# Reading a block's shifted values from memory instead of copying them on chip, and moving one rounding step

## The chip, the cores and the metric

The kernel runs on one core of a Trainium2 chip. Its engines are TensorE (PE; the loads of its weights are listed apart as PEld), VectorE (DVE), ScalarE (ACT), GpSimd (POOL) and SyncE (SP), which only issues requests; sixteen DMA engines move data between HBM and the core's SBUF. The metric is the device time of one execution in microseconds, median of several runs. Before the change it is 612.67 us (three runs, 612.29 to 614.36).

## The reference

The inputs q, k and v have shape 8 x 8 x 576 x 64 (batch, heads, positions, width). The first half is attention in a sliding window: a position sees itself and the 63 before it.

```python
mask = (rel >= 0) & (rel < 64)
scores = np.where(mask, q @ k.T / 8, -1e9)
attn = exp(scores - max) ; attn /= sum + 1e-9
x = (attn @ v)  ->  4608 rows of 512
```

The second half is a mixture of experts on these 4608 rows: a gate (logits from x and a bias by the row's modality) picks one of eight experts for each row, the row goes through that expert's two matrices (512 x 1024, relu, 1024 x 512), and the result is weighted with the gate's probability.

## The kernel before, in words

**Blocks and pairs.** The positions are cut into 72 blocks of 64; a step s of the main loop handles a pair of blocks, 2s and 2s + 1, for all eight heads (36 pairs, and a few steps behind them for what trails). A block's queries see their own block and the block before it. The work of one pair is spread over several steps, and the order on each engine is written out by hand: the loop's calls fix it.

In step s, in this order on the engines:

- TensorE multiplies probabilities with values for pair s - 2 (`values`, L709), VectorE divides by the sums into xa (`values_out`, L717 and L720), and the gate's logits follow for pair s - 3 (L738, VectorE adds the bias into lg at L743).
- TensorE makes the scores of pair s (`scores`, L653). VectorE adds the mask and finds the extreme of each head (`minima`, L667, tiles ss and mn).
- TensorE turns the exponentials of pair s - 1 (`probs_t`, L483), ScalarE copies the turned tile to pT (L688). GpSimd adds a tiny number to the sums (`sums`, L694).
- ScalarE takes the exponentials of pair s (`exps`, L679), two, three and three heads at a time; between them come its copy of the turned xa (xaT, L730), copies of turned keys (L618), and one rounding of an expert's weights (Whi, L114), whose rest VectorE takes (Wlo, L119).

**The values.** `load_v(s)` (L542, or L546 in two halves where a pair crosses two batches) requests the values of pair s into the tile vo, 128 positions x 8 heads x 64. The lower and the upper 64 partitions of vo belong to blocks 2s and 2s + 1. Block 2s + 1 is multiplied with vo as it lies: its own block in the upper half, its predecessor in the lower. Block 2s takes a second tile, ve, whose lower half holds its own block 2s and whose upper half holds its predecessor 2s - 1. `swap_upper(s - 1)` has VectorE copy the upper half of the former pair's vo into it (L556), `swap_v(s - 1)` has GpSimd copy the lower half (L550). Both happen in step s for pair s - 1; `values` reads the result in step s + 1. Two ve tiles take turns, three vo tiles.

**Experts.** From step 5 (`WEIGHTS`) on, the matrices of the two experts that get most rows are fetched in pieces of 256 KB (L103, L107, tile y) and split into a rounded part and a rest. From step 12 (`FIRST`) on, the expert matmuls of finished rows ("slots", L321 and L343) are interleaved with the attention. A generator `it` yields slot work, and `gap(it, True)` lets it advance by one piece; what the piece leaves for other engines is put on a list and issued at the next `run_later()`. For the first slot the rows xt are gathered in step 11 (`load_slot`, L217, five requests, after SyncE has fetched the row number at L204). In step 12 VectorE turns them (`x_turn`, L283). The first piece of the slot leaves `split` on the list: ScalarE rounds to xh (L195), VectorE takes the rest xl (L196).

**Queues.** SyncE issues the requests for v, q, k, weight pieces and gathered rows in program order. Each waits for its buffer. GpSimd issues the scatters of finished rows (L822). The earliest keys and queries land in the tile Whi, which is named so because the rounded weights use it later. The loop is in one large function; these are its lines on the values:

```python
        if 1 <= s < FIRST:
            swap_upper(s - 1)
        if 2 <= s < NPR + 2:
            values(s - 2)
```

Of the kernel before, what the change touches and what calls it, by code (L numbers as in the profile page):

```python
# [8 lines left out]
F32 = mybir.dt.float32  # L9
# [10 lines left out]
P = 128  # L20
W64 = 64
# [5 lines left out]
def tile_window_attn_moe(  # L27
# [12 lines left out]
    nc = tc.nc  # L40
    B, H, S, D = q.shape
# [8 lines left out]
    BPB = S // W64  # L50
# [15 lines left out]
    WEIGHTS = 5  # L66
    FIRST = 12
# [407 lines left out]
    def gap(it, wait=False):  # L475

        if next(it, "end") != "end" and not wait:
            run_later()
            tick()
# [13 lines left out]
    work = actx.enter_context(tc.tile_pool(name="work", bufs=1))  # L493
# [19 lines left out]
    v_v = v.rearrange("b h s d -> b s h d")  # L513
    vo = {}
    ve = {}
# [12 lines left out]
    def turn_bank(s):  # L528

        i = n_tp[0]  # L530
        n_tp[0] += 1
        if s < FIRST and i % 5 > 1:
            return ps_m.tile([P, 512], F32, name=("em", "y0", "y1")[i % 5 - 2])
        return tp_bank()
# [12 lines left out]

    def swap_v(p):

        nc.gpsimd.tensor_copy(out=ve[p][0:W64], in_=vo[p][0:W64])  # L550

    def swap_upper(p):
        if p not in ve:
            ve[p] = work.tile([P, H, D], F32, name="ve", bufs=2)
        if p > 0:
            nc.vector.tensor_copy(out=ve[p][W64:P], in_=vo[p - 1][W64:P])  # L556
# [126 lines left out]
    def probs_t(p, a, pp):  # L683
        ss = st[p, "s"][0][a]
        for hp in range(HP):
            turn(pp[:, hp * P:(hp + 1) * P], ss[:, hp, :])
        pT = work.tile([P, HP * P], F32, name="pT", bufs=2)
        nc.scalar.copy(out=pT, in_=pp)  # L688
        st[p, "p", a] = pT

    def sums(p):
        sm = st[p, "s"][2]
        rs = st[p, "rs"] = small.tile([P, H], F32, name="rs")
        nc.gpsimd.tensor_scalar(out=rs, in0=sm, scalar1=1e-9, scalar2=None, op0=ALU.add)  # L694
# [19 lines left out]
    def values_out(p):  # L714
        rs = st.pop((p, "rs"))
        rw = small.tile([P, 2, 2, HP], F32, name="rw")
        nc.vector.reciprocal(  # L717
            out=rw, in_=rs.rearrange("p (c g) -> p g c", g=2)[:, :, None, :].broadcast_to([P, 2, 2, HP]))
        xa = st[p, "xa"] = xas[p % XBUF]
        nc.vector.tensor_tensor(  # L720
            out=xa[:, 0:DM].rearrange("p (x d) -> p x d", d=R32),
            in0=st.pop((p, "av")).rearrange("p h d -> p (h d)").rearrange("p (x d) -> p x d", d=R32),
            in1=rw.rearrange("p g a c -> p (g a c)")[:, :, None].broadcast_to([P, 2 * H, R32]), op=ALU.mult)
# [193 lines left out]
    it = counted()  # L917
# [15 lines left out]
    def keep_warm(n):  # L933
# [11 lines left out]
        out=brow, in_=mod_bias.rearrange("(o m) e -> o m e", o=1).broadcast_to([P, 2, E]))  # L945
# [19 lines left out]
    for h in range(2):  # L965
# [3 lines left out]
        for m in range(3):  # L969
            nc.gpsimd.affine_select(  # L970
                out=masks[rows, m, own], in_=masks[rows, m, own],
# [4 lines left out]
            else:  # L976
                nc.gpsimd.affine_select(
                    out=masks[rows, m, before], in_=masks[rows, m, before],
# [5 lines left out]
    for t in xas:  # L984
# [4 lines left out]
        out=tri, in_=tri, compare_op=ALU.is_gt, fill=0.0, base=0,  # L989
# [65 lines left out]
    for c in range(NC1):  # L1055
        nc.scalar.dma_start(
            out=wg[c * R32:(c + 1) * R32],
            in_=w_gate[c * P:(c + 1) * P].rearrange("(r d) e -> d r e", d=R32))
# [14 lines left out]
    for s in range(NPR + 4):  # L1073
        j = s % GB
        if s <= FIRST:
            for f, args in at.pop(s, ()):
                f(*args)
        n_tick = 6 if s < FIRST else 5
        n_gap = 0 if s < FIRST else 4
        G = s // GB + 1  # L1080
        heads = PARTS[j] if G < NG else ()
        R = (s - 5) // GB if s >= 5 and j == 1 else -1

        def part(i):
            if not heads:
                return
            if i == 1 and quartered(G):
                turn_heads(G, *heads[1])
                return
            tp = turn_bank(s)  # L1090
            heads_t(G, *heads[i], tp)
            heads_out(tp, G, *heads[i], nc.scalar.copy if heads[i] == K1 else nc.vector.tensor_copy)

        def ranks():
            if R < 0:
                return None
            tp = turn_bank(s)
            rk = route2(R, tp)
            n = None
            if R == NG - 1 or any(R == T for T, _ in EARLY):  # L1100
                n = counts_out(tab if R == NG - 1 else pl, counts(R, tp))
            route3(R, rk)
            return n
# [4 lines that stand above are left out]
            values(s - 2)  # L1108
            if s <= FIRST:
                values_out(s - 2)  # L1110
        if 3 <= s < NPR + 3:
            logits(s - 3, turn_bank(s) if s != FIRST else ps_m.tile([P, 512], F32, name="y0"))
            if (s - 3) % GB == GB - 1:
                route1((s - 3) // GB)
        if FIRST < s < NPR + 2:
            values_out(s - 2)
        if s < NPR:
            scores(s)
            if s == FIRST:
                x_turn(fetched[0])  # L1120
                gap(it, True)
            minima(s)
            if s == FIRST - 2:
                tick(todo[0][-1] - issued[0], table=True)
        if 1 <= s <= NPR:
            if s == FIRST:
                run_later()
            if s >= FIRST:
                swap_upper(s - 1)
            swap_v(s - 1)  # L1130
            for a in range(2):
                probs_t(s - 1, a, turn_bank(s))
            sums(s - 1)
        if s < NPR:
            exps(s, (0, 1))
        if s == 0:
            first_pair(1, (both[:1], both[1:]))
            cast_bias()
        if s <= FIRST:
            if s >= 2:  # L1140
                x_t(s - 2, turn_bank(s) if s != FIRST else ps_m.tile([P, 512], F32, name="y0"))
            run_later()
            tick(2)
            if s < NPR:
                exps(s, (2, 3, 4))
            part(0)
            if s == FIRST:
                weights(s)
                gap(it, True)
            run_later()  # L1150
            tick(n_tick)
            cnt = ranks()
            exps(s, (5, 6, 7))
        else:
            gap(it, True)
            run_later()
            release()
            tick(2)
            if s < NPR:
                exps(s, (2, 3, 4))  # L1160
            if s < FIRST + 4 or s % 2:
                weights(s)
            for f, args in at.pop(s, ()):
                f(*args)
            gap(it, True)
            cnt = ranks()
            if s < NPR + 2:
                x_t(s - 2, turn_bank(s))
            part(0)
            run_later()  # L1170
            tick(n_tick)
            if s < NPR:
                exps(s, (5, 6, 7))
        if n_gap > 2:
            if FIRST <= s < FIRST + 4:
                weights(s)
            gap(it, True)
        part(1)
        run_later()
        tick(n_tick)  # L1180
        if s == WEIGHTS:
            load_weights()
        if s >= WEIGHTS:
            weights(s)
        if n_gap > 3:
            gap(it, True)
        run_later()
        if s == 1:
            select_bias()
        if s == 4:  # L1190
            nc.sync.dma_start(out=xs_blk[DUMMY:DUMMY + 2].rearrange("b p c -> p b c"), in_=padrow)
        for T, xs_ in EARLY:
            if T == R:
                plan(T, xs_, cnt)
# [24 lines left out]
    def pad_rows(e):  # L1219
# [30 lines left out]
        out=few, in_=quarters, scalar=1, op=ALU.bitwise_and))  # L1250
# [114 lines left out]
    with tc.If(trip > 0):  # L1365
        NS = N // P + E
        with ExitStack() as gctx:
# [4 lines left out]
            for st in (1, 2, 4):  # L1372
# [27 lines left out]
                out=eoff, in0=desc[0:1, 0, :], scalar1=-1.0, scalar2=float(E), op0=ALU.mult, op1=ALU.add)  # L1400
# [3 lines left out]
                out=gtab[:, :, 1], in0=rw, scalar1=float(E - 1), scalar2=None, op0=ALU.min)  # L1404

            with tc.For_i(0, trip, 1) as it:
# [8 lines left out]
                    out=xo.rearrange("p (c r d) -> p r c d", r=NR, d=R32), in_=runs_of(xt))  # L1415
# [5 lines left out]
                for c in range(NC1):  # L1421
                    wt = gen.tile([P, F], F32, name="gw1", bufs=2)
                    nc.sync.dma_start(out=wt, in_=w1_v[bass.ds(ee, 1), :, c, :].rearrange("o p f -> (o p) f"))
                    for n in range(F // 512):
                        nc.tensor.matmul(
                            out=hps[n], lhsT=xT[:, c * P:(c + 1) * P], rhs=wt[:, n * 512:(n + 1) * 512],
# [12 lines left out]
                for c2 in range(NC2 // 2):  # L1439
                    wt = gen.tile([P, 2, DM], F32, name="gw2", bufs=2)  # L1440
                    nc.sync.dma_start(
                        out=wt, in_=w2_v[bass.ds(ee, 1), :, 2 * c2:2 * c2 + 2, :].rearrange("o p c f -> (o p) c f"))
                    for i in range(2):
                        c = 2 * c2 + i
                        nc.tensor.matmul(
                            out=yp, lhsT=hT[:, c * P:(c + 1) * P], rhs=wt[:, i, :],
# [3 lines left out]
                    out=y, in0=yp, scalar1=xt[:, DM:DM + 1], scalar2=None, op0=ALU.mult)  # L1450
# [3 lines left out]
                    out=out, out_offset=bass.IndirectOffsetOnAxis(ap=oi, axis=0),  # L1454
                    in_=y, in_offset=None, bounds_check=N - 1, oob_is_err=False)
# [31 lines left out]
```

## Time and profile before

| | |
|---|---|
| median of 3 runs | 612.67 us (612.29 to 614.36) |
| profiled execution | 612.32 us, its span 610.5 us |
| busy: TensorE | 593.4 us, 97% of the span |
| busy: VectorE | 377.3 us, 62% |
| busy: ScalarE | 282.8 us, 46% |
| busy: GpSimd | 138.1 us, 23% |
| read from and written to HBM | 67.36 MB and 23.78 MB |
| steps 5 to 12, by VectorE's rows | about 35 to 84 us |

A step's start can be found in VectorE's rows by its copy into ve (L556): 34.98, 40.21, 45.10, 51.49, 57.20, 63.02 and 70.13 us are steps 5 to 11. In a row of a timeline the numbers are the start and the length in us, then engine, line, operation and tiles (out<-in); a bracket at the end tells how long the engine stood idle before and what released it. In a row of waits the numbers are us in total, times, and the longest. In a row of stretches stand the stretch, its length, and the busy time of PE, PEld, DVE, ACT and POOL with the count of instructions, then the granted clock of TensorE, the busy share of the DMA engines and GB/s.

### The profile page before, as it was taken

Reading aid. Unit: us, or ns where it says so; the run is one execution under the profiler, and the core shown is the slowest. Engines: PE = TensorE matmul, PEld = TensorE weight load, DVE = VectorE, ACT = ScalarE, POOL = GpSimd, SP = SyncE. Lnnn points to the kernel's source line nnn. Section 1 sums busy time; section 2 is a strip of 40 time slices with the busy share of each in tenths; the row PEclk is TensorE's granted clock in tenths of the full one; section 3 lists DMA queues with packets and bytes.
Section 4 is the critical chain, followed back from the end, with each engine's and each line's share of the span. In section 5 each row is a group of like instructions: output and inputs, shape, how many; then the busy total and the mean of one; then the engine's idle time right before and its main releaser. Section 6 shows DMA issues by size and latency. Waiting matters only on the chain.

```text
span 610.5 us, 17234 instructions
## 1 busy us (share of the span) xinstructions
PE 593.4 (97%) x6281; PEld 527.8 (86%) x6281; DVE 377.3 (62%) x1479; ACT 282.8 (46%) x907; POOL 138.1 (23%) x313
## 2 busy tenths in 40 slices
PE   8999889999999999999999999999999999999996
PEld 5888778889898898989898899899999999999983
DVE  3899988878777877678656465323224634765311
ACT  3899876666656564636462211111113522653110
POOL 6333332142312311321323131011001111102102
PEclk7999999999999999999999999999999999999999
DMA  9999866686776845554513033632152553687301
GB/s 171 214 237 235 209 178 169 154 196 157 192 167 153 210 108 125 145 132 82 137 53 107 36 103 122 180 116 70 34 173 77 166 172 103 202 250 253 117 18 39
DMA packets 175655, 87.95 MB, mean 144 GB/s; under 512 B 139802, under 2 KB 158288, under 8 KB 175440
## 3 DMA queue, kind: packets, MB, share of 16 engines
q1 hardware_dynamic: 166992, 67.33, 45.2%
q0 software_dynamic: 5840, 18.92, 8.4%
q8 instruction: 50, 0.82, 0.6%
q10 hardware_dynamic: 2736, 0.58, 0.5%
q14 instruction: 37, 0.30, 0.2%
HBM read 67.36 MB, written 23.78 MB: 149 GB/s over the span
## 4 chain that ended last, share of the span: by engine, by line
PE 76%; DVE 5%; ACT 2%; issue 1%; SPq 1%; DMA 1%; POOL 0%; POOLq 0%; DVEq 0%; ACTq 0%
PE y L343 29%; PE em L321 21%; PE sp L321 10%; PE tp L483 7%; PE av L709 3%; PE sp L653 3%; PE tp L738 1%; DVE xt L283 1%; ACT ss L679 1%; DVE xl L196 1%; DMA xs_scratch<-xa,idx 1%; SPq L603 1%; PE tp L393 1%; PE em L368 1%; DVE ss L667 0%
## 5 line engine op out<-in xcount | busy, mean ns | idle before, releaser
L343 PE MATMUL y<-Whi,hh 128*128 128x512 f32 x288 | 115.8, 402 | 0.0
L679 ACT ACTIVATE ss<-ss,mn 128x128 f32<-128x128 f32 x288 | 112.3, 398 | 3.5 <-DMA y<-in_moe_modality_id_dram 2.6
L343 PE MATMUL y<-Wlo,hh 128*128 128x512 f32 x288 | 112.7, 391 | 0.0
L343 PE MATMUL y<-Whi,hl 128*128 128x512 f32 x288 | 112.4, 390 | 0.0
L354 POOL DMA_INDIRECT out_dram<-y,id x36 | 38.7, 1076 | 218.3 <-DVE y L351 159.9
L330 DVE SCALAR_TENSOR_TENSOR hl<-em,hh 128x512 fp32r<-128x512 f32 x50 | 34.5, 691 | 83.9 <-ACT hh L329 83.5
L321 PE MATMUL em<-xh,Whi 128*128 128x256 f32 x400 | 81.7, 285 | 0.0
L321 PE MATMUL em<-xl,Whi 128*128 128x256 f32 x400 | 79.2, 279 | 0.0
L321 PE MATMUL em<-xh,Wlo 128*128 128x256 f32 x400 | 79.1, 279 | 0.0
L329 ACT ACTIVATE hh<-em 128x512 fp32r<-128x512 f32 x50 | 30.0, 599 | 105.1 <-PE em L321 100.1
L688 ACT COPY pT<-tp 128x512 f32<-128x512 f32 x57 | 31.2, 590 | 75.8 <-PE tp L483 75.8
L667 DVE CUSTOM_DVE_ANT_0 ss<-sp,masks 128x128 f32<-128x128 f32 x288 | 63.4, 285 | 2.4 <-PE sp L653 2.4
L321 PEld LDWEIGHTS em<-xh,Whi 128*128 128x128 f32 x400 | 62.8, 188 | 2.3
L343 PEld LDWEIGHTS y<-Whi,hl 128*128 128x128 f32 x288 | 54.1, 188 | 12.0
L343 PEld LDWEIGHTS y<-Whi,hh 128*128 128x128 f32 x288 | 54.2, 188 | 9.5 <-issue 0.8
L343 PEld LDWEIGHTS y<-Wlo,hh 128*128 128x128 f32 x288 | 54.3, 188 | 8.4
L321 PEld LDWEIGHTS em<-xh,Wlo 128*128 128x128 f32 x400 | 60.9, 188 | 0.0
L321 PEld LDWEIGHTS em<-xl,Whi 128*128 128x128 f32 x400 | 60.9, 188 | 0.0
L822 POOL DMA_INDIRECT xs_scratch<-xa,idx x36 | 36.4, 1012 | 90.5 <-DVE e_n_p L154 30.8
L679 ACT ACTIVATION_READ_ACCUMULATOR ss<-ss,mn 128x1 f32 x288 | 56.4, 196 | 0.0
L329 ACT ACTIVATE hh<-sp 128x512 fp32r<-128x512 f32 x22 | 13.2, 598 | 80.4 <-PE sp L321 80.4
L709 PEld LDWEIGHTS av<-ve,pT 128*64 128x64 f32 x576 | 36.3, 138 | 13.1 <-issue 7.8
(239 smaller groups left out, 1146.1 us busy)
## 6 DMA issues: line engine op xcount, KB each, us to landing
xt<-xs_scratch SPq DMA_DIRECT2D x72, 128.0 KB
vo<-in_v_dram SPq DMA_DIRECT2D x32, 256.0 KB
y<-in_moe_w_dram SPq DMA_DIRECT2D x32, 256.0 KB
vo<-in_moe_w_dram SPq DMA_DIRECT2D x18, 256.0 KB
ss<-in_moe_w_dram SPq DMA_DIRECT2D x18, 256.0 KB
xs_scratch<-xs_scratch SPq DMA_DIRECT2D x8, 514.0 KB
pT<-in_moe_w_dram SPq DMA_DIRECT2D x12, 256.0 KB
qk<-in_k_dram SPq DMA_DIRECT2D x22, 128.0 KB
```

The lines of the kernel that those rows point to most:

```text
L321: nc.tensor.matmul(out=hb[:, i * TP:(i + 1) * TP], lhsT=w[buf][:, c0:c0 + P], rhs=x[:, c * TP:(c + 1) * TP], start=(n == 0), stop=(n == le ...
L329: nc.scalar.activation(out=hh, in_=hb, func=AF.Relu),
L330: nc.vector.scalar_tensor_tensor(out=hl, in0=hb, scalar=0.0, in1=hh.bitcast(F32), op0=ALU.max, op1=ALU.subtract)))
L343: nc.tensor.matmul(out=sl["y", t], lhsT=h[:, i * TP + t * P:i * TP + (t + 1) * P], rhs=w[buf][:, c0:c0 + DM], start=(k == 0 and n == 0), s ...
L354: ins = nc.gpsimd.indirect_dma_start(out=out, out_offset=bass.IndirectOffsetOnAxis(ap=sl["id"][:, t:t + 1], axis=0), in_=y, in_offset=None ...
L483: nc.tensor.transpose(out=out_, in_=in_, identity=ident[p0:p0 + n, p0:p0 + n])
L653: nc.tensor.matmul(out=sp[a][c * W64:(c + 1) * W64, hp * P:(hp + 1) * P], lhsT=qT[rows, place(g + c, hp), :], rhs=kT[rows, win(c, hp), :], ...
L667: nc.vector.tensor_tensor_reduce(out=ss[a][:, hp, :], in0=sp[a][:, hp * P:(hp + 1) * P], in1=mask, scale=-1.0 / 8.0, scalar=3.0e38, op0=AL ...
L679: nc.scalar.activation(out=ss[a][:, hp, :], in_=ss[a][:, hp, :], func=AF.Exp, bias=mn[:, h:h + 1], scale=-1.0, accum_out=sm[:, h:h + 1])
L688: nc.scalar.copy(out=pT, in_=pp)
L709: nc.tensor.matmul(out=by_block(av)[c * W64:(c + 1) * W64, a, :, hp, :], lhsT=pT[:, i:i + W64], rhs=(vo if c else ve)[p][:, 2 * hp + a, :] ...
L822: ins = nc.gpsimd.indirect_dma_start(out=xs, out_offset=bass.IndirectOffsetOnAxis(ap=idx[:, j:j + 1], axis=0), in_=xg[j], in_offset=None)
```

## The change

In steps 5 to 11 a new function `load_ve(s)` allocates ve of pair s already in step s, right behind `values(s - 2)`, and has SyncE request both halves from HBM: block 2s into the lower 64 partitions, block 2s - 1 into the upper. For these seven pairs `swap_upper` and `swap_v` do nothing. The two tiles ve take turns as before, so the request waits until TensorE has read the former contents, in `values(s - 2)`.

In step 12 the first advance of the slots, `gap(it, True)`, moves from ahead of `minima` to behind `probs_t`. The rounding that it leaves on the list is then issued at a later `run_later()`.

```diff
     def swap_v(p):
 
+        if p in loaded:
+            return
         nc.gpsimd.tensor_copy(out=ve[p][0:W64], in_=vo[p][0:W64])
 
+    loaded = []
+
+    def load_ve(p):
+
+        ve[p] = work.tile([P, H, D], F32, name="ve", bufs=2)
+        for i, g in enumerate((2 * p, 2 * p - 1)):
+            s0 = (g % BPB) * W64
+            nc.sync.dma_start(out=ve[p][i * W64:(i + 1) * W64], in_=v_v[g // BPB, s0:s0 + W64])
+        loaded.append(p)
+
     def swap_upper(p):
+        if p in loaded:
+            return
         if p not in ve:
             ve[p] = work.tile([P, H, D], F32, name="ve", bufs=2)
...
             if s <= FIRST:
                 values_out(s - 2)
+            if WEIGHTS <= s < FIRST:
+                load_ve(s)
...
             if s == FIRST:
                 x_turn(fetched[0])
-                gap(it, True)
             minima(s)
...
             for a in range(2):
                 probs_t(s - 1, a, turn_bank(s))
+            if s == FIRST:
+                gap(it, True)
             sums(s - 1)
```

Two places show how the order of instructions moves. The first is SyncE's queue in steps 10 and 11, up to the first of the five requests for the gathered rows xt. (Rows into Whi are keys, rows into y weight pieces; the changed kernel's lines are 14 to 17 further down.) Before:

```order
L542 DMA vo<-in_v_dram 128x8x64
L597 DMA Whi_64<-in_k_dram 128x8x64 x2
L103 ISA
L103 DMA y<-in_moe_w_dram 128x512
L542 DMA vo<-in_v_dram 128x8x64
L204 TENSOR_LOAD rows_1490
L204 ISA x2
L217 ISA
L217 DMA xt<-xs_scratch 32x8x128
```

Changed:

```order
L542 DMA vo<-in_v_dram 128x8x64
L611 DMA Whi_64<-in_k_dram 128x8x64 x2
L561 DMA ve<-in_v_dram 64x8x64 x2
L103 ISA
L103 DMA y<-in_moe_w_dram 128x512
L542 DMA vo<-in_v_dram 128x8x64
L204 TENSOR_LOAD rows_1493
L204 ISA x2
L217 ISA
L217 DMA xt<-xs_scratch 32x8x128
```

The pair of requests for ve comes in ahead of the weight piece, and with it ahead of everything that follows on this queue: the next vo, the row number and xt. The same happens in each of steps 5 to 11.

The second place is ScalarE at the start of step 12. Before:

```order
L114 CAST Whi_65<-y 128x512
L195 CAST xh<-xt 128x512 x2
L688 COPY pT<-tp_1859 128x512
L688 COPY pT<-tp_1866 128x512
L679 ACTIVATE ss,sm<-ss,mn 128x128 x2
L730 COPY xaT<-y_1877 128x512
L679 ACTIVATE ss,sm<-ss,mn 128x128 x3
```

Changed:

```order
L114 CAST Whi_65<-y 128x512
L702 COPY pT<-tp_1849 128x512
L702 COPY pT<-tp_1856 128x512
L693 ACTIVATE ss,sm<-ss,mn 128x128 x2
L744 COPY xaT<-y_1869 128x512
L195 CAST xh<-xt 128x512 x2
L693 ACTIVATE ss,sm<-ss,mn 128x128 x3
```

The two roundings to xh move behind the two copies of turned probabilities, two exponentials and the copy xaT. On VectorE seven copies into ve are gone (steps 6 to 12), and on GpSimd seven.

## The prediction

> **What bounds the kernel now.** I read the page first, then the busy time by stretches, then the waits of the engines in the stretch that the change edits.
>
> ```profile
> PE 593.4 (97%) x6281; PEld 527.8 (86%) x6281; DVE 377.3 (62%) x1479; ACT 282.8 (46%) x907; POOL 138.1 (23%) x313
> 34.00:63.00 29.00, 27.61 (x588) 24.96 (x584) 27.39 (x153) 28.92 (x118) 8.92 (x18) 1.00 0.98 235
> 63.00:78.00 15.00, 11.99 (x215) 10.36 (x215) 14.30 (x72) 11.56 (x43) 6.63 (x11) 1.00 0.86 213
> 80.00:100.00 20.00, 19.60 (x272) 17.75 (x271) 16.74 (x68) 14.92 (x52) 2.50 (x5) 1.00 0.60 152
> ```
>
> TensorE is busy 593.4 of 610.5 us, and from 80 us on it is nearly full. Over the whole span ScalarE and VectorE look idle; that average misleads. The columns of the stretches are PE, PEld, DVE, ACT, POOL, the granted clock, the DMA share and GB/s. From 34 to 63 us (steps 5 to 9) ScalarE works 28.92 of 29.00 us: it is the bound. From 63 to 78 us (steps 10 to 12) VectorE works 14.30 of 15.00 and ScalarE only 11.56: there VectorE is the bound, and TensorE loses 3 us. Whatever these two stretches gain brings the full part forward, so it should reach the end almost whole; the part after 80 us is only shifted.
>
> The waits of ScalarE from 63 to 79 us say where it stands still, and two timelines show the last place:
>
> ```profile
> ACT xh L195 <- DVE xt L283: 1.9, 1, 1.9
> ACT ss L679 <- DVE mn L667: 0.9, 2, 0.7
> ACT ex L769 <- DVE lg L766: 0.5, 1, 0.5
> 75.56 0.60 ACT L114 CAST Whi<-y 128x512 fp32r<-128x512 f32 x1
> 78.12 1.14 ACT L195 CAST xh<-xt 128x512 fp32r<-128x512 f32 x2 [1.95 <-DVE xt L283]
> 79.16 1.06 ACT L688 COPY pT<-tp 128x512 f32<-128x512 f32 x2
> 80.12 0.41 ACT L679 ACTIVATE ss<-ss,mn 128x128 f32<-128x128 f32 x1
> 80.90 0.57 ACT L730 COPY xaT<-y 128x512 f32<-128x512 f32 x1
> 81.37 0.41 ACT L679 ACTIVATE ss<-ss,mn 128x128 f32<-128x128 f32 x1
> ...
> 70.13 0.42 DVE L556 COPY ve<-vo 64x512 f32<-64x512 f32 x1
> 76.72 0.15 DVE L743 TENSOR_TENSOR lg<-y,bias_sel 128x8 f32<-128x8 f32 x1
> 76.79 1.29 DVE L283 STREAM_TRANSPOSE xt<-xt 128x512 f32<-128x512 f32 x2
> 78.01 0.25 DVE L667 CUSTOM_DVE_ANT_0 ss<-sp,masks 128x128 f32<-128x128 f32 x1
> ```
>
> The three waits make 1.9 + 0.9 + 0.5 = 3.3 us, all for VectorE. This is the most that taking work from VectorE can bring. The gathered rows xt were there in time: VectorE turned them at 76.79 straight behind lg, with no wait.
>
> The third resource is the DMA. The rows are single stretches, and SyncE's requests:
>
> ```profile
> 20.00:34.00 14.00, 13.21 (x246) 11.89 (x248) 12.02 (x66) 12.54 (x51) 6.25 (x12) 1.00 1.01 232
> 37.00:39.00 2.00, 2.00 (x30) 1.82 (x29) 2.00 (x15) 2.00 (x8) 0.27 (x2) 1.00 0.58 103
> 39.00:69.00 30.00, 27.59 (x583) 24.71 (x579) 28.28 (x158) 28.99 (x117) 12.33 (x22) 1.00 1.01 252
> 42.00:46.00 4.00, 3.23 (x67) 2.97 (x69) 3.70 (x23) 4.00 (x17) 2.89 (x6) 1.00 1.11 282
> 69.00:71.00 2.00, 1.15 (x15) 0.85 (x8) 1.78 (x8) 2.00 (x6) 1.13 (x2) 1.00 0.14 30
> 71.00:76.00 5.00, 3.92 (x87) 3.61 (x91) 5.00 (x30) 4.32 (x19) 0.00 (x0) 1.00 0.93 208
> DMA packets 17943, 7.57 MB, mean 252 GB/s; under 512 B 16698, under 2 KB 16698, under 8 KB 17935
> 54.47 5.23 SPq L597 DMA_DIRECT2D Whi<-in_q_dram  x4
> 65.49 0.37 SPq L542 DMA_DIRECT2D vo<-in_v_dram  x1
> 69.74 2.52 SPq L217 DMA_DIRECT2D xt<-xs_scratch  x5
> 86.13 1.31 SPq L546 DMA_DIRECT2D vo<-in_v_dram  x2
> ```
>
> The DMA engines are full from 39 to 69 us: 7.57 MB in 30 us, 252 GB/s (the packet row is of that window). SyncE feels it: four requests of L597 take 5.23 us at 54.47. There are two holes: a share of 0.58 from 37 to 39 us, and 0.14 from 69 to 71, which leaves 2 x 0.86 = 1.7 us of room just ahead of the requests for xt.
>
> **The change part by part.** *Copies.* Seven half-tile copies leave each of two engines:
>
> ```profile
> L550 POOL COPY ve<-vo x36: 604/612/1048, 14.5 to 312.8; 64x512 f32<-64x512 f32 x36
> L556 DVE COPY ve<-vo x35: 424/425/532, 20.1 to 324.6; 64x512 f32<-64x512 f32 x35
> PE av L709 <- POOL ve L550: 2.4, 4, 0.8
> ```
>
> VectorE loses 7 x 0.425 = 3.0 us, GpSimd 7 x 0.612 = 4.3 us. In steps 6 to 9 the VectorE copies buy nothing directly, because ScalarE is full there; they let VectorE run ahead. TensorE's waits for GpSimd's copy (2.4 us from 20 to 80 us) cost nothing for the same reason. Before the turn of xt at 76.79 lie six copies. The three of steps 9 to 11 fall into a stretch where VectorE waits for nothing (1.3 us), the earlier three can at most double that. So VectorE would be ready to turn xt between 76.79 - 2.55 = 74.2 and 76.79 - 1.3 = 75.5, and the waits for mn and lg (1.4 us) go away.
>
> *Probabilities ahead of rounding.* In step 12 ScalarE now copies pT twice, does two exponentials and xaT, and only then rounds xh. The pT copies no longer wait for xt. If xt were turned at the same 76.79, the minima would start at 78.01 as now. An exponential can follow its minimum by 0.38 us, as in step 11:
>
> ```profile
> 71.61 0.28 DVE L667 CUSTOM_DVE_ANT_0 ss<-sp,masks 128x128 f32<-128x128 f32 x1
> 71.99 0.40 ACT L679 ACTIVATE ss<-ss,mn 128x128 f32<-128x128 f32 x1 [0.68 <-DVE mn L667]
> ```
>
> That is 78.39; then two exponentials (80.12 to 80.90, 0.78 us), xaT (0.47) and xh (78.12 to 79.16, 1.04) put the third exponential at 80.68 in place of 81.37: 0.7 us gained. VectorE's rounding of xl moves behind xh, to about 80.2, against 79.67 now; the copy that it no longer makes behind it (0.425) nearly pays for that.
>
> *The new requests.* Each of steps 5 to 11 reads two halves of 128 KB, 262 KB in rows of 256 B. A request of 64 rows costs SyncE 1.31 / 2 = 0.65 us (86.13), against 0.37 for a whole vo: 1.3 us a step, hidden while SyncE only waits for the DMA engines. The pair waits for TensorE's products of step s - 2, which stand early in step s; behind it on SyncE wait a weight piece and the next vo, both of which are used steps later. So the wait itself costs nothing; the bytes do. Six pairs lie ahead of xt. The pair of step 5 meets a hole, left by SyncE's table reads; five pairs, 1.31 MB, fall into the full stretch. Their price has two ends:
> - If the engines held the 282 GB/s of 42 to 46 us throughout, 7.57 + 1.31 = 8.88 MB would take 31.5 us in place of 30. The 1.5 us fit into the 1.7 us of room, and xt is not late.
> - At the 232 GB/s of 20 to 34 us, where nearly all is rows of 256 B, 1.31 MB takes 5.6 us; less 1.7 us of room, xt is 3.9 us late, and 5.6 late if the room is lost because SyncE first fetches the row number and then issues five requests.
>
> I take 3.5 us (1.31 MB at the mean of 252 GB/s is 5.2, less 1.7): the added rows are the short ones, and 282 stands for 4 of 30 us. xt is four requests of 131 KB; the DMA took it up at 71 us, and 0.52 MB at the 208 GB/s of 71 to 76 us takes 2.5 us, so now it lands near 74 (an estimate). 3.5 us later is 77.5, and the turn starts at 77.7 or so, 0.9 us after the present one.
>
> [...]
>
> *Sum.* The turn of xt comes 0.9 us later, the new order gives 0.7 back, and I add 0.2 us for a weight piece or a pair that comes late behind it: +0.4 us. The profiled execution took 612.32 us for its span of 610.5, and lies 0.35 us under the median of 612.67; so 612.7 for it, **613.0 us** as a median. The saving of 2 to 3 us on VectorE is exchanged for a wait for xt.
>
> **The rivals.** *The DMA takes it* (faster). The engines have shown 282 GB/s, scatters and reads overlapping. Then the turn starts between 74.2 and 75.5, 1.3 to 2.6 us early, and with 0.7 from the order the gain is 2.0 to 3.3: 609.4 to 610.7, say 610.0. Against it: the full share over 30 us, and SyncE's stretched requests.
>
> *The pair itself is late at TensorE* (slower). Products of step s need the pair of step s - 2, requested last in its step. In step 10 they run at 60.35, and there is no slack behind them:
>
> ```profile
> 60.35 0.27 PE L709 MATMUL av<-ve,pT 128*64 128x64 f32 x1
> 61.85 1.10 PE L653 MATMUL sp<-kT,qT 64*64 64x128 f32 x32
> 62.88 0.66 PE L483 MATMUL em<-ident_r,ss 128*128 128x128 f32 x4
> 63.58 0.59 ACT L688 COPY pT<-em 128x512 f32<-128x512 f32 x1
> ```
>
> TensorE's queue runs products, scores and turns back to back to 63.5, and ScalarE copies pT at 63.58. Every microsecond that the pair of step 8 lands after 60.35 is one of ScalarE's, the bound there. Its place on SyncE is just ahead of the weight piece of 53.51, and the full queue shows 5.0 us from request to landing:
>
> ```profile
> 53.51 0.37 SPq L107 DMA_DIRECT2D y<-in_moe_w_dram  x1
> xs_scratch<-xa,idx POOLq DMA_INDIRECT x6, 5.0
> ```
>
> The pairs of steps 6 and 7 push it by 2 x 262 KB / 232 = 2.3 us, so it lands near 53.5 + 2.3 + 5.0 = 60.8 (an estimate): about on time, and this case decides if it comes 1 us later still. If steps 10 and 11 lose 1 us each and xt is 4 to 5 us late, the result is near +2.5: 615.2. Against it: it needs the low rate throughout.
>
> *Given back later* (no change). The chain of waits goes at 103.63 through a scatter, whose rows the next gather reads:
>
> ```profile
> 103.63 4.14 DMA xs_scratch<-xa,idx
> ```
>
> If that second gather were held by DMA alone, a gain at step 12 would turn into TensorE idling near 118: within 0.5 us of 612.7. Against it: the scatter itself waits for earlier work that would shift along.
>
> **How the numbers follow.** Chances: my forecast 0.40 (its own range 611.2 to 614.6), the DMA takes it 0.25, the late pair 0.24, given back 0.11. A difference under 0.3% (1.8 us, so from 610.8 to 614.5) can't be told from no change here. The forecast and the fourth case lie almost wholly inside; the second gives faster, the third mostly slower. With the edges: faster 0.26, same 0.50, slower 0.24. The range takes in most of both sides: 610.0 to 615.3.
>
> **What would show it.** Right: VectorE idle before L283 (its new line the same) in step 12, ended by the DMA of xt; no wait of ScalarE for mn and lg in steps 10 and 11, but one for mn in step 12; a DMA share near 1.0 through 69 to 71 us; the exponentials directly behind pT. Wrong, faster: the turn of xt before 75.5 with no wait, and over 270 GB/s from 39 to 70. Wrong, slower: TensorE waiting for the DMA of ve before L709's products in steps 9 to 12, and ScalarE's pT copies waiting for TensorE. A wait later than 100 us that was not there before would speak for the fourth case.

## The result and the profile after

The changed kernel takes 620.21 us (median of four runs, 618.42 to 622.6) against 612.98 before: a ratio of 1.0117, 95% interval 1.007 to 1.0165. It is slower by 7.2 us, outside the predicted range of 610.0 to 615.3. The profiled execution took 618.42 us, its span 616.6.

The page's first part and the same three stretches as before:

```profile
PE 592.3 (96%) x6281; PEld 527.0 (85%) x6281; DVE 373.8 (61%) x1472; ACT 282.8 (46%) x907; POOL 132.6 (22%) x306
34.00:63.00 29.00, 22.67 (x455) 20.71 (x454) 21.27 (x131) 24.15 (x95) 6.24 (x14) 1.00 0.91 218
63.00:78.00 15.00, 10.95 (x201) 9.97 (x199) 10.90 (x67) 10.46 (x42) 2.88 (x6) 0.89 1.03 252
80.00:100.00 20.00, 18.11 (x252) 16.48 (x248) 17.98 (x76) 17.97 (x63) 5.71 (x11) 1.00 0.77 193
```

VectorE lost its 3 us of copies (377.3 to 373.8). But from 34 to 63 us, where ScalarE was full with 28.92 of 29.00 us, it now works only 24.15, and TensorE fell from 27.61 to 22.67: both stand waiting. With more asked of it the DMA moved less, 218 GB/s where before had 235, and its engines were less full, a share of 0.91 in place of 0.98. TensorE's waits from 30 to 125 us, and the three places in its timeline, say for what:

```profile
PE av L723 <- DMA ve<-in_v_dram: 5.9, 2, 4.0
PE av L723 <- ACT ss L693: 3.1, 1, 3.1
...
50.76 0.24 PE L723 MATMUL av<-ve,pT 128*64 128x64 f32 x1 [1.92 <-DMA ve<-in_v_dram]
58.83 0.24 PE L723 MATMUL av<-ve,pT 128*64 128x64 f32 x1 [3.13 <-ACT ss L693]
72.90 0.24 PE L723 MATMUL av<-ve,pT 128*64 128x64 f32 x1 [3.95 <-DMA ve<-in_v_dram]
```

These are the products of steps 8, 9 and 11, which read the pairs requested in steps 6, 7 and 9: 9.0 us of standing still. The second names ScalarE, but ScalarE had finished long before and the pair landed 0.14 us ahead of the products, so it is a DMA too (the case of a wait for several things, put down to the wrong one). ScalarE's waits from 45 to 90 us are the same stalls, passed on:

```profile
ACT pT L702 <- PE y L483: 6.8, 2, 4.5
ACT pT L702 <- PE tp L483: 2.3, 1, 2.3
ACT ss L693 <- DVE mn L681: 0.4, 2, 0.2
```

The old waits for VectorE (3.3 us for xt, mn and lg) have shrunk to 0.4 for mn. SyncE's requests and VectorE's turn of xt show the other side:

```profile
41.01 5.03 SPq L611 DMA_DIRECT2D Whi<-in_k_dram  x2
46.15 1.41 SPq L561 DMA_DIRECT2D ve<-in_v_dram  x2
76.64 3.28 SPq L217 DMA_DIRECT2D xt<-xs_scratch  x5
...
82.42 0.15 DVE L757 TENSOR_TENSOR lg<-y,bias_sel 128x8 f32<-128x8 f32 x1
82.49 1.29 DVE L283 STREAM_TRANSPOSE xt<-xt 128x512 f32<-128x512 f32 x2
```

The rows xt are requested 6.9 us later than before (76.64 against 69.74), but VectorE turns them without a wait, straight behind lg: by then the whole program is late. (The profiles do not start alike: ahead of any edit, step 5 begins 1.24 us earlier in the change than in before's, at 33.74 against 34.98. Positions are compared here without taking that off.) The pair of step 6 stands behind two key requests that SyncE needs 5.03 us to hand over, and is asked for at 46.15, 4.6 us ahead of the products that it holds up.

### The profile page after: what moved, and what is told of

Read it like the earlier page. It is cut to its first block, busy times and chain, and to the rows that moved or that the text cites. A ratio compares the mean times of both kernels' runs of the same rounds, so it can differ in the third digit from the quotient of the medians.

```text
span 616.6 us, 17235 instructions
## 1 busy us (share of the span) xinstructions
PE 592.3 (96%) x6281; PEld 527.0 (85%) x6281; DVE 373.8 (61%) x1472; ACT 282.8 (46%) x907; POOL 132.6 (22%) x306
## 4 chain that ended last, share of the span: by engine, by line
PE 79%; DVE 4%; ACT 1%; issue 1%; DMA 1%; POOL 0%; POOLq 0%; SPq 0%; DVEq 0%; ACTq 0%
PE y L343 30%; PE em L321 22%; PE sp L321 10%; PE tp L483 7%; PE av L723 4%; PE sp L667 3%; PE tp L752 2%; DVE xt L283 1%; DVE xl L196 1%; PE tp L393 1%; PE em L368 1%; ACT ss L693 1%; DMA qk<-in_k_dram 1%; DVE ss L681 1%; ACT xaT L744 0%
## 5 line engine op out<-in xcount | busy, mean ns | idle before, releaser
L723 PE MATMUL av<-ve,pT 128*64 128x64 f32 x576 | 41.1, 225 | 9.9 <-DMA ve<-in_v_dram 5.9
```

The source lines that it names most:

```text
L723: nc.tensor.matmul(out=by_block(av)[c * W64:(c + 1) * W64, a, :, hp, :], lhsT=pT[:, i:i + W64], rhs=(vo if c else ve)[p][:, 2 * hp + a, :] ...
```

## The experiments

Each kernel was compared with the kernel before on the same chip. Unless said otherwise its base is before, or the change's requests alone.

| | median us | ratio to before (95%) |
|---|---|---|
| e1 requests, old order | 622.0 | 1.0137 (1.0116 to 1.0158) |
| e2 new order, copies kept | 615.8 | 1.0031 (1.0019 to 1.0043) |
| e3 no copies, no requests | 691.44 | not comparable with before |
| e5 e3 and unread requests | 700.98 | not comparable with before |
| f1 before and six unread pairs | 624.22 | 1.0162 (1.0135 to 1.0189) |
| f4 requests a step earlier | 621.4 | 1.0122 (1.0094 to 1.015) |
| f5 upper halves only | 617.95 | 1.007 (1.0051 to 1.0088) |
| f6 copies to GpSimd | 618.97 | 1.0081 (1.0067 to 1.0095) |
| g1 the change, TensorE kept busy | 621.91 | 1.0144 (1.0115 to 1.0173) |
| g2 e2, TensorE kept busy | 614.08 | 1.0009 (0.9997 to 1.002) |
| g3 six unread pairs, 2 KB rows | 617.15 | 1.0066 (1.0042 to 1.0089) |
| f3 last two pairs only | 614.03 | 1.0014 (0.9997 to 1.003) |
| h1 f3, TensorE kept busy | 613.08 | 1.0 (0.9986 to 1.0013) |
| h2 before, TensorE kept busy | 613.55 | 1.0005 (0.9991 to 1.0018) |
| h3 upper halves out of SBUF | 620.2 | 1.0113 (1.0094 to 1.0131) |
| h4 before, busier start | 613.87 | 1.0011 (1.0001 to 1.0021) |

**The two halves of the change apart.** e1 takes the change with `gap(it, True)` back ahead of `minima`; e2 is the kernel before with only that line moved:

```diff
             if s == FIRST:
                 x_turn(fetched[0])
-                gap(it, True)
             minima(s)
...
             sums(s - 1)
+            if s == FIRST:
+                gap(it, True)
```

> Only the requests for ve in steps 5 to 11; the first advance of the slots stays ahead of the minima. Late-pair theory (TensorE stands in front of the products until the pair lands; 9.0 us of such waits in the changed profile): within 1 us of the changed kernel, 619 to 621.5. Theory that the moved advance costs: 616 or less.

> Only the moved advance in step 12; all values copied as before. By the prediction's term 0.7 us are gained: 612.0 to 612.6 where before is 612.98, that is, hardly to be told from no change. Theory that the moved advance costs: 616 or more.

The requests alone cost what the whole change costs (the intervals of e1 and of the change overlap). The new order alone loses 1.9 us. The two do not add up to the change's 7.2 us; why the second is not seen on top of the first is not shown.

**The bytes without the reader.** Both have the change's order. In e3 nothing is copied or read for steps 5 to 11, and the even blocks use vo; in e5 the pairs are requested on top, into ve tiles that nobody reads. Both leave out the right values of those blocks, and with other values the gate sends rows to other experts, which makes all that comes later another program: they are compared with each other only.

```diff
     def load_ve(p):
-        ve[p] = work.tile([P, H, D], F32, name="ve", bufs=2)
-        ...
+        ve[p] = vo[p]
         loaded.append(p)
```

> Leaves out part of the computation: in steps 5 to 11 neither copies nor requests; block 2s is multiplied with vo as it lies, so its values come out for the wrong positions. The moved advance is kept. What taking the copies away is worth with no bytes in exchange: by the waits of ScalarE for VectorE (3.3 us before) 609.5 to 610.5. If the copies were never on the path: 612 to 613.

> As the kernel with neither copies nor requests, but the seven pairs are requested at the same place of the queue into the two tiles ve, where nobody reads them; block 2s again takes vo as it lies. Late-pair theory: the bytes alone cost little, no more than 1.5 us over the kernel with neither, 610 to 612. Theory that the bytes delay everything on the queue (keys, weight pieces, gathered rows): 616 or more.

Unread pairs cost 9.5 us, and in e5 VectorE stands 8.6 us for xt. f1 shows the same with all values right: the kernel before, its copies and its order, and beside them the pairs of steps 5 to 10 into the tile xt, which lies idle until step 11.

```diff
+        t = idle_x[0][:, p % 2, 0:H * D].rearrange("p (h d) -> p h d", d=D)
+        for i, g in enumerate((2 * p, 2 * p - 1)):
+            s0 = (g % BPB) * W64
+            nc.sync.dma_start(out=t[i * W64:(i + 1) * W64], in_=v_v[g // BPB, s0:s0 + W64])
```

> The kernel before with its copies, in the old order, plus the pairs of steps 5 to 10 requested as in the change but into memory that nobody reads; all values as in the reference. If the bytes are the price (the DMA engines are full from 39 to 69 us, and whatever is next in need of the queue pays), the rows xt land late and TensorE stands still at steps 11 to 13: 5 to 9 us slower, 619 to 623 us, with no wait at the products. If the price is only that the pair itself comes late for its products, an unread pair costs nothing: 613 to 615 us.

10.3 us, more than the change itself. The first to pay are the readers of vo, which stands on the queue behind the unread pair: GpSimd's copies wait 16.0 us for it, and TensorE 6.6 us for these copies, where before has 1.6 (GpSimd's waits from 30 to 84 us, TensorE's from 30 to 125 us in f1 and then before). Then xt is late; the rows are SyncE's request, VectorE's turn and the DMA's packets from 39 to 78 us:

```profile
POOL ve L550 <- DMA vo<-in_v_dram: 16.0, 5, 6.7
PE av L720 <- POOL ve L550: 6.6, 5, 2.5
PE av L709 <- POOL ve L550: 1.6, 3, 0.8
...
78.86 2.64 SPq L217 DMA_DIRECT2D xt<-xs_scratch  x5
86.20 1.30 DVE L283 STREAM_TRANSPOSE xt<-xt 128x512 f32<-128x512 f32 x2 [7.13 <-DMA xt<-xs_scratch]
DMA packets 23303, 8.90 MB, mean 228 GB/s; under 512 B 22065, under 2 KB 22065, under 8 KB 23294
```

xt is requested 9.1 us later than before and VectorE stands 7.13 us for it. Of the 9.1 us f1 itself adds about 0.9 (an estimate): the unread pairs lie in xt's place, so the request for xt has to wait for them. From handing over vo to the request for xt SyncE stood 1.91 us in f1 and 2.19 in g3 below, where the change stood 1.05; e5, whose pairs lie in the tiles ve, stood 1.46. So the loss does not need anyone to read the pairs: the late pair is the place where the change pays, and without it whatever stands behind the pairs on the queue is late.

The 10.3 us are not all transfer. Behind the wait for xt TensorE's granted clock is 0.50, also where it is full:

```profile
90.00:94.00 4.00, 4.00 (x21) 4.00 (x20) 3.80 (x11) 4.00 (x19) 0.33 (x2) 0.50 0.01 2
```

How much of f1's price, and of e5's, is this clock was not measured.

**Earlier requests.** f4 reads all seven pairs, but asks for those of steps 6 to 9 one step earlier, two of them into xt's halves:

```diff
-            if WEIGHTS <= s < FIRST:
-                load_ve(s)
+            for p in {5: (5, 6), 6: (7,), 7: (8,), 8: (9,), 10: (10,), 11: (11,)}.get(s, ()):
+                load_ve(p)
```

> All seven pairs are read, old order, but those of steps 6 to 9 are requested one step earlier, into two more places (the idle halves of xt for 6 and 7). If lateness of the pair at the products is the price, TensorE's waits for ve (9 us in the changed kernel) fall below 2 us and the time is 611 to 614 us. If the bytes are the price, the waits at the products go, but a wait for xt or for keys comes in their place, and the time stays at 619 to 623 us.

The waits for ve in steps 8 to 11 went (two of 1.8 us in all remained there for vo). One for the pair of step 10, not asked for earlier, and one for xt came instead (TensorE's row, then VectorE's), and the time stayed:

```profile
PE av L730 <- DMA ve<-in_v_dram: 3.4, 1, 3.4
...
DVE xt L283 <- DMA xt<-xs_scratch: 4.0, 1, 4.0
```

**Half the bytes, and long rows.** f5 reads only the upper halves and leaves GpSimd its copies. g3 is f1 with the same bytes in rows of 2 KB:

```diff
-        for i, g in ((0, 2 * p), (1, 2 * p - 1)):
+        for i, g in ((1, 2 * p - 1),):
```

```diff
+            out=t, in_=v[p % 8].rearrange("h s d -> (h s d)")[0:P * H * D].rearrange("(p c) -> p c", p=P))
```

> Only the upper half of each pair of steps 5 to 11 is read (131 KB, one request); GpSimd's copy of the lower half stays; old order. If the price goes with the bytes beyond the room in the queue, it is half or less: 2 to 4 us slower than before, 615 to 617.5 us, with waits for ve of 1 to 4 us. If it goes with the waiting request of a step rather than its size, it is as in the version with the loads alone: 620 to 622 us.

> As the version with six unread pairs and the copies kept (624.2 us), but each pair's 262 KB is read in rows of 2 KB by one request of 128 rows instead of two requests with rows of 256 B. If the number of short rows sets the price, it shrinks to a third or less: 614 to 617 us. If the bytes set it, it stays at 620 to 625 us.

Half the bytes cost 4.0 us. The long rows cost 3.9 where the short ones cost 10.3, so the same number of bytes has no fixed price. What sets it is not told apart: g3 also asks with one request a pair where f1 asks with two, and reads other places of v. Of the pairs of steps 9 and 10, SyncE hands over g3's two requests in 1.31 us in all and f1's four in 3.78, and f5, with six requests of short rows and half the bytes ahead of xt, lost as much as g3 (4.0 against 3.9). The length of the rows and the number of requests both fit. SyncE's request for xt and the packets from 39 to 76 us in g3:

```profile
75.92 2.50 SPq L217 DMA_DIRECT2D xt<-xs_scratch  x5
DMA packets 19598, 9.42 MB, mean 255 GB/s; under 512 B 17548, under 2 KB 17548, under 8 KB 19589
```

With long rows the mean rate holds (255 GB/s, before 252); with short ones it drops to 228. But f1's engines were also less full in that stretch, a share of 0.95 against 0.99 in g3 and 1.01 before.

**Only the last pairs.** f3 requests the pairs of steps 10 and 11 alone (`if FIRST - 2 <= s < FIRST`).

> Only the pairs of steps 10 and 11 are read, old order; the copies of steps 5 to 9 stay. At the price that six unread pairs showed (10.3 us for 1.57 MB, 1.7 us a pair) two pairs cost 3.4 us, less what VectorE's relief brings (1 to 2 us): 614.5 to 617 us. If the prediction's room of 1.7 us from 69 to 71 us takes them up, nothing is lost and VectorE's relief shows: 611 to 613.5 us.

No difference can be told. SyncE's requests:

```profile
64.09 1.87 SPq L561 DMA_DIRECT2D ve<-in_v_dram  x2
66.97 0.18 SPq L542 DMA_DIRECT2D vo<-in_v_dram  x1
71.01 2.52 SPq L217 DMA_DIRECT2D xt<-xs_scratch  x5
74.78 1.51 SPq L561 DMA_DIRECT2D ve<-in_v_dram  x2
```

Only the pair of step 10 stands ahead of xt; that of step 11 comes behind it. xt is requested 1.3 us later than before, but SyncE had handed over all that stands ahead of it by 67.15 us and then stood for 3.86. Before stood 3.88 at the same place, 2.1 of it for VectorE's lg ahead of the row number and 1.1 for a scatter; what f3 stood for is not told apart.

**TensorE's clock.** In the changed kernel the granted clock is 0.57 from 74 to 78 us, behind the 3.95 us stall; in e2 it falls too, to 0.68 from 84 to 88 us, behind a wait of 1.85. (The stretches of the change, then of e2, then of before.)

```profile
70.00:74.00 4.00, 1.10 (x39) 1.14 (x39) 2.04 (x9) 2.97 (x13) 0.42 (x2) 1.00 1.04 253
74.00:78.00 4.00, 4.00 (x59) 3.65 (x55) 2.23 (x15) 0.53 (x1) 0.00 (x0) 0.57 1.05 253
```

```profile
80.00:84.00 4.00, 2.34 (x12) 1.90 (x13) 2.76 (x8) 4.00 (x16) 1.02 (x2) 0.89 0.45 170
84.00:88.00 4.00, 4.00 (x47) 3.87 (x48) 2.81 (x9) 3.22 (x10) 0.28 (x1) 0.68 0.38 105
```

```profile
76.00:80.00 4.00, 2.14 (x34) 1.73 (x25) 3.91 (x22) 2.05 (x5) 3.52 (x8) 1.00 0.97 303
84.00:88.00 4.00, 3.60 (x88) 3.17 (x85) 2.93 (x7) 3.04 (x8) 0.34 (x1) 1.00 0.65 187
```

g1 and g2 fill the stalls with matmuls on constants, whose result is overwritten (in g1 also 4, 8 and 12 ahead of the products of steps 8, 9 and 11):

```diff
             hb = sl["hb"]
+            if k == i == 0 and not warmed:
+                warmed.append(1)
+                for _ in range(8):
+                    nc.tensor.matmul(out=hb, lhsT=ones, rhs=ones[:, None, :].broadcast_to([P, 4, P]), ...)
```

> The version with the new order alone and 8 matmuls on constants in front of the first expert matmuls of step 12, where TensorE waits for xh from 79.8 to 81.7 us and the granted clock then is 0.50 from 83.4 to 86.8 us. If the half clock is what makes the new order 1.9 us slower than before, the time is that of before, 613.5 to 614.5 us. If it is the later xh itself (1.5 us later first matmul), it stays at 615.3 to 616.3 us.

> The changed kernel with matmuls on constants in TensorE's stalls, so that the granted clock does not fall after them: 4, 8 and 12 in front of the products of steps 8, 9 and 11, and 8 in front of the first expert matmuls of step 12. In the changed kernel's trace TensorE stands still for 3.95 us before step 11's products and then runs at a granted clock of 0.50 to 0.67 from 74 to 78 us; the version with the loads alone shows three such stretches of 3.4 us. If that is a part of the loss, these stretches go and the time falls by 1.7 to 4 us, to 616 to 618.5 us. If the clock's fall costs nothing (TensorE is not the bound there), it stays at 619.5 to 622 us.

g2 keeps the full clock and is level with before: by the two ratios the half clock was about 1.3 of the 1.9 us that the new order lost. Its stretch, to be set beside e2's:

```profile
84.00:88.00 4.00, 4.00 (x94) 3.73 (x92) 3.14 (x10) 3.22 (x11) 0.73 (x1) 1.00 0.46 120
```

g1 has the full clock (1.00) from 34 to 100 us as well and is no faster than the change. So the half clock is not what the change lost, unless the constants, which took 7.6 us of TensorE, cost as much as they saved.

The same filling, seven matmuls ahead of `part(0)` in step 12, on f3 (h1) and on before (h2, the control):

> The version that reads only the pairs of steps 10 and 11 (614.0 us, level with before), with 7 matmuls on constants in TensorE's stall of step 12 (77.7 to 79.6 us). Its trace had half the clock from 80.2 to 87.8 us, with TensorE full. If that hides the gain of VectorE's relief, the time falls to 611 to 612.5 us; if the two pairs give no gain in the first place, it stays at 613.5 to 614.5 us.

> The control: the kernel before with the same 7 matmuls on constants. Its trace had the full clock after that stall, so there is nothing to win, and the matmuls fit into the stall: 613 to 614 us, within 0.2% of before.

f3's profile had the clock at 0.57 from 80 to 88 us, h1's has 1.00. h1 is level with before and with its control: what two pairs cost and what VectorE's relief of two copies brings come to nothing together, within 0.14%. A small price and a small gain that cancel would look the same.

**Two other ways to relieve VectorE.** f6 gives the upper copies of blocks 9 to 11 to GpSimd; h3, on h2, gives them to a DMA out of vo in SBUF.

```diff
-            nc.vector.tensor_copy(out=ve[p][W64:P], in_=vo[p - 1][W64:P])
+            copy = nc.gpsimd.tensor_copy if 9 <= p < FIRST else nc.vector.tensor_copy
+            copy(out=ve[p][W64:P], in_=vo[p - 1][W64:P])
```

(h3: `nc.sync.dma_start` in place of `nc.gpsimd.tensor_copy`.)

> No bytes at all: in blocks 9 to 11 the copy of the upper half goes to GpSimd instead of VectorE (0.61 us in place of 0.43), everything else as before. It measures what VectorE's relief alone is worth in steps 10 to 12. By the prediction's first step, VectorE reaches the turn of xt up to 1.3 us earlier: 611.0 to 612.5 us beside 613 before. If GpSimd's second copy is late for the products or VectorE is not the bound there: 613 to 614 us.

> The control, with the upper halves of blocks 9 to 11 copied by a DMA out of vo in SBUF (64 rows of 2 KB, 131 KB a step) instead of by VectorE; GpSimd's copies stay. 0.26 MB before xt at the 255 GB/s of the version with long rows is 1.0 us, within the room of 1.7 us. If VectorE's relief is worth something: 611.5 to 612.8 us; if not, or if the DMA is late for the products: 613.3 to 615 us.

Both are slower, and in both copies come late. In f6 GpSimd's first copy runs 3.49 us behind two scatters that it had issued, by its row released by a scatter's transfer; TensorE stands 5.00 us (its row), and the clock is then at 0.50:

```profile
68.77 0.61 POOL L557 COPY ve<-vo 64x512 f32<-64x512 f32 x1 [3.49 <-DMA xs_scratch<-xa,idx]
...
70.09 0.37 PE L710 MATMUL av<-ve,pT 128*64 128x64 f32 x1 [5.00 <-POOL ve L550]
...
70.00:74.00 4.00, 3.91 (x72) 3.88 (x76) 1.11 (x3) 0.00 (x0) 1.90 (x6) 0.50 0.76 177
```

In h3 it is the DMA, although the bytes are few and xt is requested only 1.2 us later than before (TensorE's waits, two of them, then SyncE's request):

```profile
PE av L710 <- DMA ve<-vo: 6.7, 2, 3.4
...
70.96 2.53 SPq L217 DMA_DIRECT2D xt<-xs_scratch  x5
```

So late operands alone can cost nearly as much as the change lost (ratios of 1.0081 and 1.0113 against 1.0117); h3's request comes one step before its use, the change's two. Neither kernel says what VectorE's relief is worth by itself.

**The start.** h4 gives before 7 in place of 3 matmuls on constants at the start (`WARM = 8, 7`).

> The kernel before with 7 instead of 3 matmuls on constants in the stall at 6.4 us. Its trace had half the clock from 8.8 to 15.5 us. If that stretch is the reason that the changed kernel's profile, with the full clock there, was 1.2 us ahead in step 2, the median falls by 0.5 to 1.2 us, to 612.2 to 613.2 us; if the matmuls are in the way or the clock does not matter there, it stays at 613.5 to 614.5 us.

Not faster. In its profile the low clock moved from 8 to 16 us (before 0.58 and 0.56 in its two halves) to 16 to 20 us (0.58), and another came from 80 to 84 us (0.60, before 1.00); so what the clock at the start is worth stays open.

## Why the prediction was wrong

**The price of the bytes: the step that failed.** I took five pairs at the mean of 252 GB/s, less 1.7 us of room: xt 3.5 us late. Measured, its request came 6.9 us late in the change, and with six unread pairs 9.1 us (f1), with the time 10.3 us longer. Three things were off. The rate: I priced the added bytes alone, but the whole stretch moved more slowly, 230 GB/s in the change by the next row; 7.57 + 1.31 MB at that rate take 38.6 us in place of 30 (an estimate). Part of this is that the mixture with the added rows runs lower: f4's engines were full from 39 to 77 us (a share of 1.00) and moved 233 GB/s. Part is that the engines stood: their share was 0.93 in the change and 0.95 in f1, against 1.01 before. The count: I left out the pair of step 5 for a hole; the rule below fits better with it in, which is argued and not shown. The unit: counted in packets, the stretches agree better than in bytes. Before, 17943 packets took 30 us, 598 a microsecond; f1 598 (23303 in 39), and the change, from 39 to 76 us:

```profile
DMA packets 22398, 8.52 MB, mean 230 GB/s; under 512 B 21236, under 2 KB 21236, under 8 KB 22390
```

22398 in 37 us is 605. A pair is 1024 rows of 256 B, 1.7 us at 600 a microsecond (an estimate from these rows). Less the room of 1.7 us, six pairs ahead of xt make 8.5 us (f1 measured 9.1, about 0.9 of it its own), six halves 3.4 (f5: requested at 73.41, 3.7 late), one pair nothing (f3: 1.3, behind a stand of SyncE as long as before's). The fit is no proof. By the same rule g3's 768 added packets would fit into the room, and its request for xt came 6.2 us late; g3's stretch ran at 530 a microsecond, and the stretch from 20 to 34 us before, without scatters, at 787. Whether rows, requests or SyncE's order set the price stays open: for as many bytes f1 cost 10.3 us and g3 3.9, but g3 also has half the requests.

**"The wait itself costs nothing."** Wrong from step 8 on. I looked for the late pair in step 10 only and put it at 60.8 us, about on time. That sum had SyncE request the pair of step 8 at 55.8 us, where the change requested it at 59.86, and took a scatter's 5.0 us for the landing of a read. The change waited in steps 8, 9 and 11, 9.0 us. The rival "the pair itself is late at TensorE" named the place, the waits and their heirs (ScalarE's pT copies) rightly; it had 0.24 and 2.5 us because it "needs the low rate throughout", and over the change's whole stretch the rate was low (230 GB/s). As a cause it is only half right: f1 and f4 show that without those waits the time is lost elsewhere, at xt and, in f1, at vo. The next vo behind the pair, which I had as "used steps later", was not safe either: in f1, where GpSimd still copies from it, the copies stood 16.0 us for it.

**The new order.** I had it win 0.7 us; it lost 1.9 (e2). The sum let the exponentials start at 78.39 with both pT copies done. ScalarE's rows in e2 show that the copies themselves were not ready:

```profile
78.52 0.58 ACT L688 COPY pT<-tp 128x512 f32<-128x512 f32 x1 [2.09 <-PE y L483]
79.26 0.59 ACT L688 COPY pT<-tp 128x512 f32<-128x512 f32 x1 [0.16 <-PE y L483]
...
80.99 1.14 ACT L195 CAST xh<-xt 128x512 fp32r<-128x512 f32 x2
```

They wait for TensorE's turns, so little moves forward, while xh moves from 78.12 to 80.99 and the first expert matmuls wait 1.85 us for it. The half clock that followed (0.50 from 84 to 86 us) had no term in the sum: the prediction read the clock of before (1.00) as a given.

**VectorE's relief.** Its copies are gone, the waits for mn shrank and that for xt vanished; but VectorE also had the time of TensorE's stalls, so it is not shown that the relief did this. Its worth, up to 2.6 us in the prediction, was never seen. With two copies gone and two pairs read, h1 is level with before. What all seven would bring with no price is open: no tried way was free.

**The other rivals.** "The DMA takes it" needed 282 GB/s throughout and is refuted: the change moved 230. So is "Given back later": TensorE's products of step 18 start 5.3 us later than before (141.4 against 136.1 us) in a profile whose span is 6.1 us longer, so the loss stays.

**What was right.** That the loss would come from the queue, the doubt about short rows (f4's 233 GB/s), and that the two edits are priced apart: e1's 8.1 us is the change's 7.2 within the intervals.

## What to carry to other kernels

Before on-chip copies are replaced by reads, count the packets and requests that are to go through an already full stretch, not only the bytes, and do not price them at the stretch's mean rate: what is added can lower the rate for everything in it (252 GB/s before, 230 in the change, 228 in f1). When the queue is behind, an earlier request can just move the wait to the next reader (f4: 4.0 us for xt, and 621.4 us in all): measure the price with reads that nobody uses, into a place that nobody needs. And where TensorE is made to stand still, look at its clock behind the stall (0.57 from 74 to 78 us behind the change's 3.95 us, and 1.00 from 80 to 84 in before, which worked only 2.14 us from 76 to 80): a stall has to be priced with it.

## What was not expected of the hardware

- The granted clock was 0.50 behind some stalls, for stretches of about 3.4 us (the change, from 74.3 to 77.7; e2, from 83.1 to 86.5), about twice that (f3, from 80.6 to 87.4) or three times (f1, from 84.7 to 94.9); these edges are worked out from the clock of stretches of 1 us (an estimate). In the 4 us windows of these profiles it fell behind 1.10 us of work in four (the change) and 0.00 (f6); before worked 2.14 from 76 to 80 and kept 1.00. What decides is not shown. TensorE need not stand still all through the stretch ahead of a fall: in e2 it worked 1.56 of the 3.41 us ahead (as long as the fall lasted), and its longest wait was 1.85 us.
- With TensorE kept busy on constants for 1.9 us (8 matmuls) the clock was 1.00 from 84 to 88 us in g2, where e2 had 0.68; the two ratios, 1.0009 and 1.0031, differ by about 1.3 us.
- A short copy by DMA within SBUF (131 KB in 2 KB rows) was late for its reader by up to 3.4 us, twice (h3).
